# Attention with a gated unit on one core: heads of Q and K interleaved on partitions, stacked operands copied by row pairs

## The chip, the cores and the metric

The kernel runs on one core of one Trainium2 chip. The metric is the time of one execution on the device in microseconds (us), the median of several runs. Beside it stands one profiled execution, whose trace gives the duration of every instruction, what each engine waited for, and what the DMA queue did. TensorE (PE) multiplies matrices, VectorE (DVE), ScalarE (ACT) and GpSimd (POOL) work element by element, and SyncE (SP) issues all the transfers of this kernel.

## What is computed

Attention over queries that are averaged in pairs, and a gated unit over all heads of a batch. Cut to what matters:

```python
# q, k, v: (8, 8, 1152, 64) fp32
q_pool = q.reshape(B, H, S // 2, 2, D).mean(axis=3)          # 576 queries
scores = np.matmul(q_pool, k.transpose(0, 1, 3, 2)) / np.sqrt(D)
attn = np.exp(scores - np.max(scores, axis=-1, keepdims=True))
x = np.matmul(attn / (attn.sum(-1, keepdims=True) + 1e-9), v)  # to (8, 576, 512)
h = np.maximum(x @ w_in, 0.0)                                # w_in (512, 1024)
u, g = h[..., :512], h[..., 512:]
g = (g - mean(g)) / np.sqrt(var(g) + 1e-6)
g = np.einsum('ts,bsd->btd', w_spatial, g) + b_spatial[None, :, None]
out = (u * g) @ w_out                                        # (8, 576, 512)
```

## The kernel before

The 64 heads are worked off in 32 pairs of heads. For a pair, Q and K lie transposed in SBUF, 64 rows (the head's dimension) for each head, 128 rows for both: head 0 on the lower 64 partitions, head 1 on the upper 64. fp32 products are made of fp16 pieces: `prep` scales Q and K, rounds them to a head (qn[:, 0], kn) and keeps the rest (qn[:, 1], and for K a tile klo).

The scores of one tile of 128 keys by 512 queries are two matmuls into one bank. The first (L904) contracts over 128 rows: khi holds kn of one head twice, once on each half of the partitions, and qhi holds qn's head on one half and qn's rest on the other. The second (L905) contracts over 66 rows: klo holds K's rest on 64 rows and the constant -2**15 on two more, and X (xq) holds qn's head on 64 rows and on two more (rows D and D + 1, D = 64) the maximum of each query's scores, split into two fp16 numbers. The maximum is thus subtracted by the matmul. These stacked operands have to be written across partitions, which only a transfer does: `copies` (L681 to L683) makes ten of them for a pair, `prep` two for klo (L671, L672) and, from the third pair on, two for Z (tile qz, L646 and L647), and `shift` two for the rows of maxima (L732, mr into X). That is sixteen for a pair. Q's rest and its copies go through one tile qn; kn has two, klo three (NSET), the others two.

`maxima` finds the maxima: a matmul of kn with Z (L699), where Z holds qn's head with the other head's rows set to zero, so that one matmul over all 128 rows gives one head's products; DVE reduces each bank of 384 keys (L705). `shift` then takes the maximum over the banks (L718), subtracts and scales (L719), splits it in two (L722, L723), turns it by a matmul (L727), casts it to mr (L729) and sends it to X.

The main loop goes over the pairs i. During attention(i), the generators maxima(i + 1), prep(i + 2), split_v(i + 1) and the conversion of the weights run in steps beside it, and from pair 5 on the gated unit. At the start of a step come copies(i + 1) and the loads of pair i + 2. The first two pairs are prepared ahead of the loop and call `copies` from `prep`.

The program's order on each engine is not the order in which it is written: `Order.pin` lists all instructions, finds what each depends on, gives each a cost, and draws up one order for each of the five engines by a list schedule, SP's transfers among them. Each engine then runs strictly in that order. `Order.access` (L68) tells which rows and bytes of a tile an operand covers. On SP each transfer also waits until the eighth transfer before it has landed, since eight semaphores are handed round.

## Time and profile before

| | |
|---|---|
| median of 3 runs | 1170.97 us (1170.41 to 1171.24) |
| profiled execution | 1171.14 us |
| its span on the core | 1169.4 us |
| mean granted clock of TensorE | 0.997 |
| transfers by SP | 139.44 MB, 42.4% of the 16 DMA engines' time |

The span is what the trace covers; 1.7 us of the execution lie outside it. A row of a view names the line in the kernel, the engine, the operation and its tiles (written tile, arrow, read tiles). Rows that end in "<-" and a name tell what an idle engine waited for; the figures are the total in us, how often, and the longest. Rows of the chain hold a start, a length and the work that the end of the execution depended on at that time.

### The profile page before, as it was taken

To read this page: it belongs to the slowest core of one execution; us is meant where nothing else is said; L and a number is where in the kernel's file an instruction comes from. 1 tells how busy PE (TensorE), PEld (TensorE's weight loads), DVE (VectorE), ACT (ScalarE), POOL (GpSimd) and SP (SyncE) were. 2 spreads that over 40 slices of the span, in tenths; PEclk is the share of its full clock that TensorE was granted. 3 is DMA by queue.
4 is the path that set the end of the run, shared out by engine and by line. 5 is a ranking of instruction groups with operands and counts; after the bars stand their busy time and mean duration, and the time that the engine had idled before them with its cause. 6 is when DMAs were issued, how large, how long until landed. Compare 5 with 4: busy or idle time off the path is not lost.

```text
span 1169.4 us, 33651 instructions
## 1 busy us (share of the span) xinstructions
PE 1132.8 (97%) x13412; PEld 715.2 (61%) x13412; DVE 838.8 (72%) x2095; ACT 896.4 (77%) x1700; POOL 884.5 (76%) x766
## 2 busy tenths in 40 slices
PE   4999999999999999999999999999999999999998
PEld 1766676666566666666666666666666666665453
DVE  6899878898856877786668677865668676822644
ACT  7997899788886879797787977878777867754433
POOL 5765789879898889999987978888788977873000
PEclk9999999999999999999999999999999999999999
DMA  9855354345453344654533544366443432121002
GB/s 294 233 181 157 95 161 149 92 118 152 128 162 110 106 126 135 169 135 131 153 109 87 159 117 130 95 178 171 120 114 88 119 97 50 36 65 37 1 1 82
DMA packets 93757, 141.59 MB, mean 121 GB/s; under 512 B 36704, under 2 KB 52832, under 8 KB 93600
## 3 DMA queue, kind: packets, MB, share of 16 engines
q1 hardware_dynamic: 93600, 139.44, 42.4%
q8 instruction: 105, 1.72, 0.6%
q14 instruction: 52, 0.43, 0.1%
HBM read 81.20 MB, written 9.44 MB: 78 GB/s over the span
## 4 chain that ended last, share of the span: by engine, by line
PE 84%; DVE 10%; DMA 3%; ACT 2%; issue 1%; SPq 0%; DVEq 0%; ACTq 0%
PE pss L905 9%; PE pm L699 9%; PE pss L904 9%; PE pw L1002 7%; PE pw L1105 7%; PE pw L1149 6%; PE pw L1063 6%; PE o L807 5%; PE o L818 5%; PE o L813 5%; DVE mt L705 3%; PE o L800 2%; PE pss L921 1%; PE pm L878 1%; PE pm L876 1%; PE pss L1002 1%
## 5 line engine op out<-in xcount | busy, mean ns | idle before, releaser
L930 POOL TENSOR_TENSOR pt<-pt 128x512 f16<-128x512 f32 x546 | 597.6, 1113 | 128.8 <-ACT pt L910 126.7
L705 DVE TENSOR_REDUCE mt<-pm 128x1 f32<-128x384 f32 x762 | 404.4, 551 | 119.9 <-PE pm L699 114.5
L910 ACT ACTIVATE pt<-pss,esc 128x512 f32<-128x512 f32 x576 | 388.6, 694 | 112.0 <-PE pss L905 95.9
L699 PE MATMUL pm<-kn,qz 128*128 128x384 f16 x762 | 239.4, 329 | 6.9 <-DVE mt L705 4.5
L904 PE MATMUL pss<-qhi,khi 128*128 128x512 f16 x576 | 219.0, 381 | 4.2 <-ACT pt L910 1.8
L905 PE MATMUL pss<-xq,klo 66*128 66x512 f16 x576 | 218.5, 384 | 3.3 <-DMA xq<-mr 3.3
L807 PEld LDWEIGHTS <-pt 128*128 128x128 bf16 x2184 | 124.7, 98 | 61.4 <-issue 3.2
L807 PE MATMUL o<-vp,pt 128*128 128x65 f16 x2184 | 160.1, 193 | 0.5 <-DVE xm L826 0.4
L813 PE MATMUL o<-vp,pt 128*128 128x64 f16 x2184 | 158.8, 193 | 0.0
L818 PE MATMUL o<-vp,pt 128*128 128x65 f16 x2184 | 158.0, 193 | 0.2
L818 PEld LDWEIGHTS <-pt 128*128 128x128 f16 x2184 | 121.8, 98 | 52.3 <-POOL pt L930 1.8
L699 PEld LDWEIGHTS <-qz 128*128 128x128 f16 x864 | 83.8, 99 | 62.4 <-issue 19.1
L813 PEld LDWEIGHTS <-pt 128*128 128x128 bf16 x2184 | 105.6, 98 | 3.6 <-issue 0.2
L1002 PE MATMUL pw<-wi_h,xg 128*128 128x512 f16 x248 | 92.0, 379 | 0.0
L1063 PE MATMUL pw<-xg,wi_h 128*128 128x512 f16 (+2 forms) x368 | 82.9, 311 | 0.0
L930 POOL TENSOR_TENSOR ptl<-ptl 128x1152 f16<-128x1152 f32 x32 | 69.2, 2163 | 17.2 <-ACT ptl L926 17.2
L1149 PE MATMUL pw<-wo_h,vv 128*128 128x512 f16 x224 | 81.2, 379 | 0.5 <-DVE vv L402 0.3
L1105 PE MATMUL pw<-ws_h,vv 128*128 128x512 f16 x216 | 79.1, 379 | 0.7 <-DVE u L1115 0.7
L595 POOL TENSOR_TENSOR vp<-vt,vp 128x576 f16<-128x576 f32 x54 | 68.1, 1266 | 13.7 <-ACT vp L399 13.6
L905 PEld LDWEIGHTS <-klo 66*128 66x128 f16 x576 | 56.1, 98 | 34.6 <-issue 6.2
L926 ACT ACTIVATE ptl<-pss,esc 128x256 f32<-128x256 f32 (+1 forms) x128 | 64.5, 504 | 15.2 <-PE pss L921 15.2
L656 POOL TENSOR_TENSOR klo<-kt,kn 128x640 f16<-128x640 f32 (+1 forms) x54 | 72.7, 1348 | 0.0
(229 smaller groups left out, 2386.0 us busy)
## 6 DMA issues: line engine op xcount, KB each, us to landing
vt<-in_v_dram SPq DMA_DIRECT2D x56, 576.0 KB
qt<-in_qT_dram SPq DMA_DIRECT2D x32, 576.0 KB
khi<-kn SPq DMA_DIRECT2D x128, 144.0 KB
kt<-in_kT_dram SPq DMA_DIRECT2D x31, 576.0 KB
qhi<-qn SPq DMA_DIRECT2D x128, 72.0 KB
out_dram<-row SPq DMA_DIRECT2D x24, 256.0 KB
xq<-qn SPq DMA_DIRECT2D x64, 72.0 KB
klo<-klo SPq DMA_DIRECT2D x32, 144.0 KB
```

Source lines behind the costliest of these rows:

```text
L699: nc.tensor.matmul(pm[:, :W], lhsT=Z[:, t * P : (t + 1) * P], rhs=kn[:, n * NB : (n + 1) * NB, :], start=True, stop=True,)
L705: nc.vector.reduce_max(out=mt[:, t, n : n + 1], in_=pm[:, :W], axis=AX.X)
L807: nc.tensor.matmul(o[:, t], lhsT=top[:, cols], rhs=vp[:, D : D + D1], start=c == 0 and t == 0, stop=False, skip_group_check=True,)
L813: nc.tensor.matmul(o[:, t, 0:D], lhsT=top[:, cols], rhs=vp[:, 0:D], start=False, stop=False, skip_group_check=True)
L818: nc.tensor.matmul(o[:, t], lhsT=rst[:, cols], rhs=vp[:, D : D + D1], start=False, stop=c == NC - 1, skip_group_check=True,)
L904: nc.tensor.matmul(o, lhsT=khh[:, h, c, :], rhs=qhl[:, h, q], start=True, stop=False)
L905: nc.tensor.matmul(o, lhsT=KL[0:KR, h, c, :], rhs=X[0:KR, h, q], start=False, stop=True)
L910: nc.scalar.activation(pt, ps, AF.Exp, bias=0.0, scale=esc)
L930: nc.gpsimd.tensor_sub(t.bitcast(F16)[..., 0::2], t, t.bitcast(BF16)[..., 1::2])
L1002: nc.tensor.matmul(ph, lhsT=xa[:, cc, c0 : c0 + P], rhs=wa[:, cc, DH:DF], start=n == 0, stop=n == 3 * NCC - 1,)
L1063: nc.tensor.matmul(pu[:, : z - a], lhsT=wa[:, cc, fc * P : (fc + 1) * P], rhs=xa[:, cc, a:z], start=n == 0, stop=n == 3 * NCC - 1,)
L1105: nc.tensor.matmul(pv, lhsT=l, rhs=r[:, 0:MAIN], **fl)
```

## The change

Q's and K's rows are laid out as (dimension, head) in place of (head, dimension): row 2d + h holds dimension d of head h. The host hands them over in that order, and the loads stay whole tiles.

- The rows of one head are now every second partition. `copies` fills qhi of one head with one transfer from 64 rows, each of which gives two rows of the target (qn's head and its rest lie side by side in a row), and khi of one head with one transfer that reads each of the 64 rows of kn twice. X takes both heads in one transfer, and klo too. That is six transfers for what took ten and klo's two.
- K's rest goes to a tile of its own, kl, of which there is one; klo is filled from it by the last transfer of `copies`, is two tiles instead of three, and its rows of constants are set once at the start. prep's sums of squares use kn for their discarded output, not klo.
- Z is still written by two transfers, of every second row. For the first two pairs DVE multiplies all 128 rows by a column of ones and zeros (own), which is built from the identity matrix at the start, instead of copying 64 rows. Z is set to zero as a whole.
- The two rows of maxima go in one transfer (L733) instead of two.

A pair so has nine transfers (two for Z, six in `copies`, one for the maxima). `Order.access` is adapted to a step between rows.

```diff
@@ -73,8 +73,9 @@
             return None
         size = self.SIZE[ap.dtype]
         dims = [list(d) for d in ap.ap]
-        row, parts = dims[0]
+        row = math.prod(ap.tensor.shape[1:]) * self.SIZE[ap.tensor.dtype] // size
         first, off = divmod(ap.offset, row)
+        parts = dims[0][0] // row * (dims[0][1] - 1) + 1
         run, g, ext = size, 0, 0
         for s, n in sorted((d[0] * size, d[1]) for d in dims[1:] if d[1] > 1 and d[0]):
             if s == run and not g:
@@ -277,7 +278,7 @@
 def attn_sgu_kernel(ctx: ExitStack, tc: tile.TileContext, qT, kT, v, w_in, w_spT, b_sp, w_out, out):
     nc = tc.nc
     P = 128
-    B, NHP, _, D, _, S = qT.shape
+    B, NHP, D, _, _, S = qT.shape
     NC = kT.shape[4]
     NP = B * NHP
     KEYS = NC * P
@@ -345,9 +346,10 @@
 
     NSET = 3
     kns = [const.tile([P, NC, P], F16, name=f"kn{i}") for i in range(2)]
-    klo = [const.tile([P, 2, NC, P], F16, name=f"klo{i}") for i in range(NSET)]
+    kls = [const.tile([P, NC, P], F16, name=f"kl{i}") for i in range(1)]
+    klo = [const.tile([P, 2, NC, P], F16, name=f"klo{i}") for i in range(2)]
     for t in klo:
-        nc.gpsimd.memset(t[D:KR, 1], -MROW)
+        nc.gpsimd.memset(t[D:KR], -MROW)
     qns = [const.tile([P, 2, S], F16, name=f"qn{i}") for i in range(1)]
     xq = [const.tile([P, 2, S], F16, name=f"xq{i}") for i in range(2)]
     khi = [const.tile([P, 2, NC, P], F16, name=f"khi{i}") for i in range(2)]
@@ -355,8 +357,10 @@
 
     qz = [const.tile([P, 2, S], F16, name=f"qz{i}") for i in range(2)]
     for t in qz:
-        nc.gpsimd.memset(t[D:P, 0], 0.0)
-        nc.gpsimd.memset(t[0:D, 1], 0.0)
+        nc.gpsimd.memset(t, 0.0)
+    own = const.tile([P, 2], F32, name="own")
+    for h in range(2):
+        nc.vector.reduce_sum(out=own[:, h : h + 1], in_=ident[:, h::2], axis=AX.X)
 
     wi_h = const.tile([P, NCC, DF], F16, name="wi_h")
     wi_l = const.tile([P, NCC, DF], F16, name="wi_l")
@@ -508,13 +512,13 @@
 
         b, hp = divmod(i, NHP)
         qt = ld.tile([P, KEYS], F32, name="qt", bufs=2)
-        nc.sync.dma_start(out=qt, in_=qT[b, hp].rearrange("h d r s -> (h d) (r s)"))
+        nc.sync.dma_start(out=qt, in_=qT[b, hp].rearrange("d h r s -> (d h) (r s)"))
         state[i] = {"qt": qt}
 
     def load_k(i):
         b, hp = divmod(i, NHP)
         kt = mo.tile([P, NT * DH], F32, name="u")[:, :KEYS] if i == 1 else ld.tile([P, KEYS], F32, name="kt")
-        nc.sync.dma_start(out=kt, in_=kT[b, hp].rearrange("h d c p -> (h d) (c p)"))
+        nc.sync.dma_start(out=kt, in_=kT[b, hp].rearrange("d h c p -> (d h) (c p)"))
         state[i]["kt"] = kt
 
     v_first = {}
@@ -606,14 +610,14 @@
     def prep(i):
         st = state[i]
         kt, qt = st["kt"], st["qt"]
-        X, KL, khh, qhl, Z, kn, qn = (x[i % len(x)] for x in (xq, klo, khi, qhi, qz, kns, qns))
+        X, KL, khh, qhl, Z, kn, qn, kl = (x[i % len(x)] for x in (xq, klo, khi, qhi, qz, kns, qns, kls))
         k0 = kt.rearrange("p (c k) -> p c k", k=P)
         q0, q1 = qt[:, 0:S], qt[:, S:]
-        st.update(qhl=qhl, khh=khh, X=X, KL=KL, kn=kn, qn=qn, Z=Z)
+        st.update(qhl=qhl, khh=khh, X=X, KL=KL, kn=kn, qn=qn, Z=Z, kl=kl)
         first = i == 0
         (nc.vector if i < FIRST else nc.gpsimd).tensor_add(q0, q0, q1)
         sq = sm.tile([P, 2], F32, name="sq", bufs=2)
-        junk = KL[:, 0].rearrange("p c k -> p (c k)")
+        junk = kn.rearrange("p c k -> p (c k)")
         square_sum(sq[:, 0:1], kt, junk)
         yield
         square_sum(sq[:, 1:2], q0, junk[:, :S])
@@ -634,17 +638,16 @@
                 out=lnp, in0=lnp, scalar1=math.log(PEXP) / ESC, scalar2=2.0 ** 29, op0=ALU.mult, op1=ALU.min
             )
 
-        lower, upper = slice(0, D), slice(D, P)
         if not first:
             factors()
             yield
         head(qn[:, 0], q0, s_q)
         if i < FIRST:
-            nc.vector.tensor_copy(out=Z[lower, 0], in_=qn[lower, 0])
-            nc.vector.tensor_copy(out=Z[upper, 1], in_=qn[upper, 0])
+            for h in range(2):
+                nc.vector.tensor_scalar_mul(Z[:, h], qn[:, 0], own[:, h : h + 1])
         else:
-            nc.sync.dma_start(out=Z[lower, 0], in_=qn[lower, 0])
-            nc.sync.dma_start(out=Z[upper, 1], in_=qn[upper, 0])
+            for h in range(2):
+                nc.sync.dma_start(out=Z[h::2, h], in_=qn[h::2, 0])
         if not first:
             rest(qn[:, 1], q0, s_q, qn[:, 0])
             yield
@@ -653,34 +656,33 @@
                 nc.scalar.activation(k0[:, a:z], k0[:, a:z], AF.Copy, bias=0.0, scale=s_k)
                 yield
                 head(kn[:, a:z], k0[:, a:z], 1.0)
-                nc.gpsimd.tensor_sub(KL[:, 0, a:z], k0[:, a:z], kn[:, a:z])
+                nc.gpsimd.tensor_sub(kl[:, a:z], k0[:, a:z], kn[:, a:z])
             else:
                 head(kn[:, a:z], k0[:, a:z], s_k)
                 yield
                 if not first:
-                    rest(KL[:, 0, a:z], k0[:, a:z], s_k, kn[:, a:z])
+                    rest(kl[:, a:z], k0[:, a:z], s_k, kn[:, a:z])
             yield
         if first:
             rest(qn[:, 1], q0, s_q, qn[:, 0])
             factors()
             for a, z in ((0, 5), (5, NC)):
                 nc.scalar.activation(k0[:, a:z], k0[:, a:z], AF.Copy, bias=0.0, scale=s_k)
-                nc.gpsimd.tensor_sub(KL[:, 0, a:z], k0[:, a:z], kn[:, a:z])
+                nc.gpsimd.tensor_sub(kl[:, a:z], k0[:, a:z], kn[:, a:z])
         if i < FIRST:
             copies(i)
-        nc.sync.dma_start(out=KL[lower, 1], in_=KL[upper, 0])
-        nc.sync.dma_start(out=KL[D:KR, 0], in_=KL[D:KR, 1])
         yield
 
     def copies(i):
 
-        khh, kn, qhl, qn, X = (state[i][n] for n in ("khh", "kn", "qhl", "qn", "X"))
+        khh, kn, qhl, qn, X, KL, kl = (state[i][n] for n in ("khh", "kn", "qhl", "qn", "X", "KL", "kl"))
+        flat = "p c k -> p (c k)"
         for h in range(2):
-            rows = slice(h * D, (h + 1) * D)
-            for r in range(2):
-                nc.sync.dma_start(out=qhl[r * D : (r + 1) * D, h], in_=qn[rows, r])
-                nc.sync.dma_start(out=khh[r * D : (r + 1) * D, h], in_=kn[rows])
-            nc.sync.dma_start(out=X[0:D, h], in_=qn[rows, 0])
+            twice = kn[h::2].rearrange(flat).unsqueeze(1).to_broadcast([D, 2, KEYS])
+            nc.sync.dma_start(out=qhl[:, h], in_=qn[h::2])
+            nc.sync.dma_start(out=khh[:, h].rearrange(flat), in_=twice)
+        nc.sync.dma_start(out=X[0:D].rearrange("p h s -> p (h s)"), in_=qn[:, 0])
+        nc.sync.dma_start(out=KL[0:D].rearrange("p h c k -> p (h c k)"), in_=kl.rearrange(flat))
 
     def maxima(i):
         st = state[i]
@@ -727,9 +729,8 @@
         nc.tensor.matmul(t, lhsT=mc, rhs=ident_h, start=True, stop=True)
         mr = sm.tile([2 * NT, P], F16, name="mr", bufs=2)
         nc.vector.tensor_copy(out=mr[: 2 * n], in_=t[: 2 * n])
-        for r in range(2):
-            rows = X[D + r : D + r + 1].rearrange("p h s -> p (h s)")
-            nc.sync.dma_start(out=rows[:, a * P : z * P], in_=mr[r * n : (r + 1) * n])
+        rows = X[D : D + 2].rearrange("p h s -> p (h s)")
+        nc.sync.dma_start(out=rows[:, a * P : z * P], in_=mr[: 2 * n])
         yield
 
 
@@ -1286,6 +1287,7 @@
     NC = S2 // 128
 
     kT = k.reshape(B, H // 2, 2, 128, NC, D).transpose(0, 1, 2, 5, 4, 3)
+    qT, kT = (x.swapaxes(2, 3) for x in (qT, kT))
     return {
         "qT": qT,
         "kT": kT,
```

The planner draws up a new order. On SP, from the last copies of pair 0 (counted from 0) up to its first rows of maxima (mr into xq), before the change; klo_109 and xq_116 are operands of pair 0, qt and kt the loads of pair 2:

```order
L682 DMA khi_118<-kn_107 64x1152
L683 DMA xq_116<-qn_115 64x576
L671 DMA klo_109<-klo_109 64x1152
L511 DMA qt<-in_qT_dram 128x1152
L517 DMA kt<-in_kT_dram 128x1152
L672 DMA klo_109<-klo_109 2x1152
L455 DMA vv<-in_w_in_dram 128x2x512
L732 DMA xq_116<-mr 1x5x128 x2
```

And at the same place with the change, from the first copy of pair 0 on (klo_110 and xq_115 are pair 0's):

```order
L684 DMA xq_115<-qn_114 64x2x576
L683 DMA khi_117<-kn_107 128x1x1152
L682 DMA qhi_119<-qn_114 128x1x576 x2
L683 DMA khi_117<-kn_107 128x1x1152
L515 DMA qt<-in_qT_dram 128x1152
L685 DMA klo_110<-kl_109 64x2x1152
L521 DMA kt<-in_kT_dram 128x1152
L459 DMA vv<-in_w_in_dram 128x2x512
L544 DMA vt<-in_v_dram 128x2x576
L733 DMA xq_115<-mr 2x5x128
```

A load of V (vt) now stands ahead of the first rows of maxima, and the load of Q ahead of the copy to klo.

On DVE, from the reduction over the banks to the cast to mr of pair 2 (near 80 us in the trace of before) and somewhat beyond, before:

```order
L718 TENSOR_REDUCE pw<-mt 128x9
L719 TENSOR_SCALAR pw<-pw,lnp 128x9
L402 SCALAR_TENSOR_TENSOR klo_109<-kt,qks,kn_108 128x512
L722 CAST wide_135<-pw 128x9
L723 TENSOR_TENSOR wide_135<-pw,wide_135 128x9
L425 TENSOR_SCALAR vv<-vv 128x1024
L729 CAST mr<-pw 18x128
L705 TENSOR_REDUCE mt<-pm 128x1
L402 SCALAR_TENSOR_TENSOR vp_101<-xg,vs,vp_101 128x9x64
```

With the change:

```order
L720 TENSOR_REDUCE pw<-mt 128x9
L883 TENSOR_SCALAR xt<-pm,dent 64x64 x2
L721 TENSOR_SCALAR pw<-pw,lnp 128x9
L724 CAST wide_135<-pw 128x9
L725 TENSOR_TENSOR wide_135<-pw,wide_135 128x9
L406 SCALAR_TENSOR_TENSOR kl_109<-kt,qks,kn_108 128x512
L731 CAST mr<-pw 18x128
L395 TENSOR_REDUCE vt<-vsq 128x1
L406 SCALAR_TENSOR_TENSOR vp_101<-xg,vs,vp_101 128x9x64
L433 SCALAR_TENSOR_TENSOR vv<-vv 128x1024
L707 TENSOR_REDUCE mt<-pw 128x1
```

A step of the weights' conversion (L425, 1024 columns) has left the stretch ahead of the cast, two products for xt have come into it, and no reduction of maxima (mt) follows the cast at once.

On DVE again, at the same place of the next pair (near 112 us), before:

```order
L402 SCALAR_TENSOR_TENSOR wi_l<-u,wvs,wi_h 128x2x512
L882 TENSOR_SCALAR xt<-pm,dent 64x64 x2
L718 TENSOR_REDUCE pw<-mt 128x9
L719 TENSOR_SCALAR pw<-pw,lnp 128x9
L722 CAST wide_136<-pw 128x9
L723 TENSOR_TENSOR wide_136<-pw,wide_136 128x9
L402 SCALAR_TENSOR_TENSOR wi_l<-u,wvs,wi_h 128x2x512
L729 CAST mr<-pw 18x128
```

With the change:

```order
L720 TENSOR_REDUCE pw<-mt 128x9
L707 TENSOR_REDUCE mt<-pw 128x1
L721 TENSOR_SCALAR pw<-pw,lnp 128x9
L406 SCALAR_TENSOR_TENSOR kl_109<-kt,qks,kn_107 128x512
L724 CAST wide_136<-pw 128x9
L725 TENSOR_TENSOR wide_136<-pw,wide_136 128x9
L406 SCALAR_TENSOR_TENSOR vp_102<-xg,vs,vp_102 128x9x64
L731 CAST mr<-pw 18x128
L406 SCALAR_TENSOR_TENSOR wi_l<-u,wvs,wi_h 128x2x512
```

The two wide steps of the weights (wi_l) stood on both sides of the reduction; one now stands behind the cast, and a step of K's rest (kl) and one of V (vp) ahead of it.

## The prediction

> **What bounds the kernel now.** I read the page's totals first, then the windows of the stages, then the chain and the waits of TensorE.
>
> ```profile
> span 1169.4 us, 33651 instructions
> PE 1132.8 (97%) x13412; PEld 715.2 (61%) x13412; DVE 838.8 (72%) x2095; ACT 896.4 (77%) x1700; POOL 884.5 (76%) x766
> PE 84%; DVE 10%; DMA 3%; ACT 2%; issue 1%; SPq 0%; DVEq 0%; ACTq 0%
> ```
>
> TensorE is busy 97% of the span and holds 84% of the chain that ended last. The change takes no matmul away, so it can only recover what TensorE loses, 36.6 us of idle time (1169.4 - 1132.8), and what it loses by running slowly. The next view gives each stretch of the span with its length and busy times; the figure behind POOL is the granted clock, the last two are DMA.
>
> ```profile
> core 0: us, PE busy (x) PEld busy (x) DVE busy (x) ACT busy (x) POOL busy (x), PEclk, DMA share, GB/s
> 0.00:20.00 20.00, 8.02 (x24) 2.55 (x25) 12.86 (x30) 14.85 (x32) 9.57 (x20) 1.00 0.91 300
> 20.00:40.00 20.00, 15.32 (x123) 8.71 (x122) 16.55 (x47) 16.07 (x34) 10.08 (x9) 1.00 0.90 271
> 84.00:88.00 4.00, 2.24 (x29) 1.28 (x30) 3.58 (x8) 3.50 (x9) 1.19 (x2) 1.00 0.53 138
> 88.00:92.00 4.00, 4.00 (x37) 2.64 (x36) 4.00 (x8) 3.53 (x8) 1.95 (x2) 0.57 0.10 25
> 112.00:116.00 4.00, 3.30 (x37) 2.14 (x34) 3.90 (x9) 2.57 (x5) 1.04 (x1) 1.00 0.34 78
> 116.00:120.00 4.00, 2.75 (x18) 1.44 (x18) 4.00 (x11) 0.44 (x1) 0.00 (x0) 0.86 0.24 56
> 120.00:124.00 4.00, 4.00 (x47) 2.67 (x45) 2.99 (x7) 3.17 (x7) 2.09 (x2) 0.72 0.00 0
> 940.00:960.00 20.00, 20.00 (x246) 12.94 (x244) 15.62 (x37) 14.97 (x29) 16.08 (x14) 1.00 0.30 77
> ```
>
> The last row stands for most of the span: nothing is lost there. The loss sits in three places: the first 40 us (16.7 us idle), the stall at 84 to 88 (1.76 us idle), and the one at 112 to 120 (0.70 + 1.25). Behind each of the latter two the granted clock falls, to 0.57 and to 0.86 and 0.72, which costs 4 x 0.43 = 1.7 us and 4 x (0.14 + 0.28) = 1.7 us more. A stall here is paid twice. Which waits involve a transfer:
>
> ```profile
> PE pss L905 <- DMA xq<-mr: 3.3, 3, 1.9
> PE pss L904 <- DMA khi<-kn: 1.3, 1, 1.3
> 13.12 5.37 DMA khi<-kn
> 18.58 1.01 PE pss L904 x2
> ...
> 23.20 5.38 DMA xq<-mr
> 28.62 1.01 PE pss L905 x2
> ...
> 83.33 2.79 DMA xq<-mr
> 86.26 0.59 PE L905 MATMUL pss<-xq,klo 66*128 66x512 f16 x2 [1.09 <-DMA xq<-mr]
> 87.83 0.38 PE L904 MATMUL pss<-qhi,khi 128*128 128x512 f16 x1 [0.55 <-ACT pt L910]
> ...
> 474.65 3.44 DMA xq<-mr
> ```
>
> All of TensorE's waits on transfers are 4.6 us: one for the stacked K copies, three for the rows of maxima (mr into X, before the first L905 of a pair).
>
> **The change part by part.** *The start.* L905 at 28.62 is the gate: TensorE runs in order, so what is behind it waits too. It waits for the first rows of maxima, issued at 23.20 and 5.38 us under way, because they queue behind what was issued earlier. The rate of that queue:
>
> ```profile
> 3.00:9.00 6.00, 0.16 (x1) 0.00 (x0) 2.29 (x7) 2.73 (x7) 4.68 (x8) 1.00 1.02 395
> 14.50:18.50 4.00, 2.76 (x6) 0.48 (x5) 4.00 (x9) 3.94 (x10) 0.25 (x1) 1.00 0.99 212
> ```
>
> Loads over 128 rows move at 395 GB/s, the 64-row copies at 212, with the queue full in both. Ahead of the first rows of maxima the order of the change puts one more load (vt, 128 x 1152 of 4 bytes, 0.59 MB: 1.5 us at 395) and a klo copy of 64 x 2304 of 2 bytes, 0.29 MB, in place of half as much (+0.7 us at 212). Against that, 0.88 MB of khi and qhi go in 128-row transfers. No row shows an SBUF copy of that form: between 212 and 395 GB/s it saves 0 to 1.9 us. I take 395, since the loads are the only other 128-row transfers here: 1.5 + 0.7 - 1.9 = **+0.3 us**, at worst +2.2. L904 comes 1.0 us earlier by the same rate (it needs half of them) and gains nothing while L905 stays.
>
> The Trainium skill, "SBUF — State Buffer", section on the DMA port swizzle, says that a transfer's rate goes by how many of 16 ports its partitions reach, 64 consecutive ones reaching 8. The 212 against 395 agree; every second partition reaches all 16, so the rule gives the +0.3, while destinations X and klo, 64 consecutive rows, stay slow.
>
> The other edits of the start are covered:
>
> ```profile
> L643 DVE COPY qz<-qn x2: 292/297/302, 9.9 to 23.8; 64x576 f16<-64x576 f16 x2
> L1036 DVE TENSOR_SCALAR row<-vv,mv,rs x37: 527/544/1266, 220.9 to 1107.4; 128x512 f32<-128x512 f32 x37
> L350 POOL MEMSET klo<- x3: 1052/1101/1169, 1.9 to 4.0; 2x1152 f16 x3
> 7.50 0.34 POOL L407 MEMSET wide<- 128x128 f16 x2
> ```
>
> The masked products into qz take between 0.30 us each, as the copies did, and 0.59 (527 ns for 512 columns, scaled to 576); I take 0.35, nearer the f16 row. At worst 0.6 us on two, hidden by the queue that holds the copies until 14.5; without that cover it would be 0.6. The klo memsets are four of L350's size, not three: POOL ends 1.1 us later than 7.84, before qz is needed at 9.9. The two sums of ident are two reductions that DVE does before the first load lands.
>
> *The second gate, 86.26.*
>
> ```profile
> 82.44 1.64 SPq L732 DMA_DIRECT2D xq<-mr  x2
> 78.85 0.23 DVE L719 TENSOR_SCALAR pw<-pw,lnp 128x9 f32<-128x9 f32 x1
> 82.14 0.27 DVE L729 CAST mr<-pw 18x128 f16<-18x128 f32 x1
> L425 DVE TENSOR_SCALAR vv<-vv 128x1024 int32<-128x1024 int32 x2 | 2.6, 1298 | 0.0
> L429 DVE SCALAR_TENSOR_TENSOR vv<-vv 128x1024 int32<-128x1024 int32 x1 | 1.5, 1508 | 0.0
> L402 DVE SCALAR_TENSOR_TENSOR klo<-kt,qks,kn 128x640 f16<-128x640 f32 (+1 forms) x4 | 4.2, 1061 | 0.0
> L402 DVE SCALAR_TENSOR_TENSOR vp<-xg,vs,vp 128x576 f16<-128x576 f32 x4 | 4.0, 1000 | 0.0
> L402 DVE SCALAR_TENSOR_TENSOR wi_l<-u,wvs,wi_h 128x1024 f16<-128x1024 f32 x2 | 4.2, 2082 | 0.0
> L882 DVE TENSOR_SCALAR xt<-pm,dent 64x64 f32<-64x64 f32 x6 | 1.7, 277 | 0.0
> ```
>
> Two issues took 1.64 us; one takes half, 0.8 less until the rows are off. In DVE's new order L425 (1.30) no longer stands ahead of the cast to mr, two xt (0.28 each) do: 0.7 us earlier. Together 1.5 us, more than the wait of 1.09; the 0.55 behind it follows from it. So 1.76 idle and 1.7 of clock, 3.4 us, can go. Late next is DVE: around the cast (0.27) it now has 5.5 us without a reduction of maxima (two xt, kl 1.06, vp 1.00, L429 1.51, five short ones at up to 0.23), where it had 3.6 (klo 1.06, L425 1.30, four short ones). TensorE's L699 waits for those reductions, 0 to 1.9 us; I take the middle, 1.0. **-2.4 us** (-3.4 to 0).
>
> *The third, 109 to 124.* DVE held 5.9 us without a reduction (two wi_l of 2.08, two xt, mr, four short ones). Now kl and vp stand ahead of mr and one wi_l behind it: 2.08 + 1.06 + 1.00 + 0.27 and three short ones, 5.1. I count the difference, **-0.8 us**, and keep 0 and -3.6 (0.70 + 1.25 idle, 1.7 clock) as ends.
>
> *The one at 474.* A single issue brings the rows 0.8 us earlier than its wait (3.3 less 1.9 and 1.09, some 0.4 us) needs: **-0.4 us**.
>
> The stacked row pair has a price the other way:
>
> ```profile
> L732 SPq DMA_DIRECT2D xq<-mr x68: 612/747/1191, 22.3 to 1032.8; - x68
> ```
>
> 68 issues become 34. The trace gives no price of a 256-byte row. Between nothing and that of a 2304-byte row (a khi copy, 0.147 MB at 212 GB/s, is 0.7 us for 64 rows on 16 engines, 0.17 each) lies 0 to 1.6 us if one engine must do nine in turn. I take nothing; those copies are the nearest row, but of nine times the bytes.
>
> The Trainium skill, "DMA: Bandwidth & Descriptors", section on why a DMA increments its semaphore by 16, says the number of engines is the largest up to 16 that divides the outer sizes of both sides. For two rows from 18 that is 2 engines, where nine rows had 9: it speaks against this edit, and no run here shows it; it gives the 1.6 us.
>
> *The rest of the span.* Seven issues fewer a pair, about 4 us of SP, bring nothing where SP is not waited for: TensorE loses nothing there. kl rests in one tile, so its next write waits for the copy to klo. Behind that write on DVE (POOL in later pairs) stand maxima, or the rests of pt that L818 needs.
>
> ```profile
> 57.74 1.21 SPq L683 DMA_DIRECT2D xq<-qn  x1
> 74.05 1.11 DVE L402 SCALAR_TENSOR_TENSOR klo<-kt,qks,kn 128x640 f16<-128x640 f32 x1
> ```
>
> The klo copy goes out right behind the X copy, which ended its issue at 58.95; the next write came at 74.05, 15 us later. With the longest transfer above (5.4 us) 9 us are left: nothing.
>
> Sum: 0.3 - 2.4 - 0.8 - 0.4 = **-3.3 us** from the profiled execution's 1171.14 (span and 1.7 us around it), 0.2 above the median of the runs, 1170.97. That is **1167.8 us**.
>
> **The rivals.** *Both stalls go, clock and all* (-3.4 - 3.6 - 0.4, nothing at the start): 1163.7. For it: a stall avoided keeps the clock. Against: DVE is busy 4.00 of 4 us around both, and its work is the same. *Hidden or moved*: TensorE's freed time goes into new waits of the same size on DVE, whose order the planner drew anew: 1171, within 1.5. For it: 10% of the chain is DVE. *Slower at the start*: if a transfer's time goes by its rows, not by what they reach, the copies save nothing (+2.2) and the row pair on two engines costs 1.6 less the 0.8 of an issue, so L905 opens 3.0 us later and the second gate gains nothing: 1174.1. It decides from a copy rate below about 250 GB/s. Against it: 395 GB/s for loads of 128 rows. *kl binds*: a write that waits 1 us in each of 30 pairs gives 1200; against it the 9 us.
>
> **How the numbers follow.** Forecast 0.47 (its own range 1165 to 1170), both stalls 0.12, hidden 0.23, slower start 0.13, kl 0.05. A measurement of this kernel can tell about 0.2%, 2.3 us. Of the forecast about 0.34 lies beyond that; with the 0.12 and 0.02 of the hidden case faster is 0.48. Same is 0.13 + 0.18, and slower 0.13 + 0.05 + 0.03. The range from 1163.5 to 1173.3 leaves out kl, most of the slower start and a little of the best case.
>
> **What would show it.** Right: L905's first wait ends between 28 and 30; no wait on a transfer near 86, the clock at 1.00 there; DMA above 300 GB/s while khi and qhi move. Wrong: the first rows of maxima landing after 30, a granted clock below 1 at a new place between 60 and 140, or POOL or DVE waiting on the klo copy.

## The result and the profile after

| | before | after |
|---|---|---|
| median of 6 executions each | 1170.69 us (1167.22 to 1172.39) | 1178.84 us (1176.34 to 1183.16) |
| profiled execution | 1171.14 us | 1179.84 us |
| its span | 1169.4 us | 1177.7 us |
| granted clock of TensorE, mean | 0.997 | 0.995 |

The ratio is 1.0077 (95% interval 1.0052 to 1.0101): slower by 8.2 us, and 5.5 us above the upper end of the range. The page of the changed kernel, totals and chain:

```profile
span 1177.7 us, 33350 instructions
PE 1133.5 (96%) x13412; PEld 715.6 (61%) x13412; DVE 854.6 (73%) x2097; ACT 899.4 (76%) x1700; POOL 883.4 (75%) x763
PE 78%; DVE 11%; ACT 5%; DMA 3%; issue 1%; POOL 1%; SPq 0%; ACTq 0%; DVEq 0%; POOLq 0%
```

TensorE's work is the same, and so is POOL's. DVE is busy 15.8 us longer (838.8 before) for two instructions more: its instructions took longer. Where TensorE lost the time is read from the windows of both kernels (start and end, length, busy time of PE, PEld, DVE, ACT and POOL, granted clock, DMA). First before, then after:

```profile
80.00:100.00 20.00, 17.87 (x193) 11.94 (x192) 18.51 (x38) 16.84 (x34) 10.54 (x9) 0.91 0.50 145
100.00:140.00 40.00, 37.26 (x429) 26.39 (x427) 36.33 (x88) 30.41 (x53) 26.01 (x21) 0.96 0.42 126
140.00:320.00 180.00, 173.81 (x2190) 113.97 (x2190) 152.38 (x362) 156.89 (x297) 152.12 (x123) 1.00 0.46 133
520.00:540.00 20.00, 20.00 (x280) 13.33 (x278) 11.96 (x36) 18.46 (x37) 19.79 (x20) 1.00 0.64 179
```

```profile
80.00:100.00 20.00, 19.37 (x233) 14.12 (x233) 18.88 (x45) 19.97 (x46) 13.68 (x11) 1.00 0.64 175
100.00:140.00 40.00, 38.29 (x490) 28.71 (x489) 38.78 (x91) 33.93 (x59) 30.10 (x23) 1.00 0.52 164
140.00:320.00 180.00, 171.38 (x2132) 111.32 (x2129) 152.91 (x357) 154.71 (x293) 149.24 (x121) 0.99 0.43 132
520.00:540.00 20.00, 12.41 (x157) 8.12 (x153) 14.72 (x13) 8.77 (x18) 12.68 (x13) 0.83 0.48 155
```

What a window loses is its length less busy time times clock. From 80 to 140 it was 3.7 + 4.2 us and is 0.6 + 1.7, so 5.6 us are won: both stalls went, and the clock no longer falls. From 140 to 320 it was 6.2 and is 10.3, so 4.1 are given back. From 520 to 540 nothing was lost, and now 9.7. Those three come to 8.2 of the 8.3 us between the spans; the clock is given to a hundredth, which leaves the middle one uncertain by some 0.9 us. What is to be explained is one place, so its timeline is read next, DVE and PE first, then POOL (start, length, instruction; in brackets the idle time before it):

```profile
520.73 0.27 DVE L731 CAST mr<-pw 18x128 f16<-18x128 f32 x1
520.93 9.28 DVE L406 SCALAR_TENSOR_TENSOR qn<-qt,qks,qn 128x576 f16<-128x576 f32 x1
530.12 1.01 DVE L707 TENSOR_REDUCE mt<-pw 128x1 f32<-128x384 f32 x2
...
531.65 0.48 PE L701 MATMUL pm<-kn,qz 128*128 128x384 f16 x1 [7.59 <-DVE mt L707]
```

```profile
521.05 1.16 POOL L659 TENSOR_TENSOR kl<-kt,kn 128x512 f16<-128x512 f32 x1
522.17 3.04 POOL L931 TENSOR_TENSOR pt<-pt 128x512 f16<-128x512 f32 x3
525.16 1.24 POOL L599 TENSOR_TENSOR vp<-vt,vp 128x576 f16<-128x576 f32 x1
526.36 2.04 POOL L931 TENSOR_TENSOR pt<-pt 128x512 f16<-128x512 f32 x2
528.35 1.23 POOL L599 TENSOR_TENSOR vp<-vt,vp 128x576 f16<-128x576 f32 x1
```

One instruction of DVE, the rest of Q of pair 17, takes 9.28 us, though it needs 0.8 where nothing holds it up (the gated kernel below shows it). When it starts, POOL is in the last 0.1 us of an instruction; eight more follow end to end, the last until 529.58, and the rest ends at 530.21, 0.63 us later: it did its work only when POOL had nothing left to do. Meanwhile the reductions of maxima stand behind it on DVE, TensorE's L701 behind those, and everything else behind L701.

The Trainium skill, "SBUF — State Buffer", section "Who interferes with whom", says that a DVE instruction with two inputs from SBUF and a GpSimd instruction that reads SBUF contend for one shared pair of ports, that this is an exclusive lock, and that whichever issues first has it for its whole instruction while the other is blocked. The trace agrees that one waits for the other; that the wait goes on over eight further instructions is not in that rule.

### The profile page after: what moved, and what is told of

Its sections match the earlier page's. It is cut to its first block, busy times and chain, and to the rows that moved or that the text cites. A ratio compares the mean times of both kernels' runs of the same rounds, so it can differ in the third digit from the quotient of the medians.

```text
span 1177.7 us, 33350 instructions
## 1 busy us (share of the span) xinstructions
PE 1133.5 (96%) x13412; PEld 715.6 (61%) x13412; DVE 854.6 (73%) x2097; ACT 899.4 (76%) x1700; POOL 883.4 (75%) x763
## 4 chain that ended last, share of the span: by engine, by line
PE 78%; DVE 11%; ACT 5%; DMA 3%; issue 1%; POOL 1%; SPq 0%; ACTq 0%; DVEq 0%; POOLq 0%
PE pm L701 9%; PE pss L906 9%; PE pss L905 9%; PE pw L1150 6%; PE pw L1106 6%; PE pw L1064 6%; PE pw L1003 6%; DVE mt L707 5%; PE o L808 5%; PE o L819 4%; PE o L814 4%; DVE qn L406 2%; ACT pt L911 2%; PE pm L877 1%; PE pm L879 1%; PE pss L1003 1%
## 5 line engine op out<-in xcount | busy, mean ns | idle before, releaser
L701 PE MATMUL pm<-kn,qz 128*128 128x384 f16 x762 | 239.5, 330 | 14.2 <-DVE mt L707 13.5
L905 PE MATMUL pss<-qhi,khi 128*128 128x512 f16 x576 | 219.1, 381 | 3.1 <-ACT pt L911 1.2
L906 PE MATMUL pss<-xq,klo 66*128 66x512 f16 x576 | 218.3, 383 | 3.5 <-DMA xq<-mr 3.5
L701 PEld LDWEIGHTS <-qz 128*128 128x128 f16 x864 | 83.9, 99 | 64.0 <-issue 10.7
L906 PEld LDWEIGHTS <-klo 66*128 66x128 f16 x576 | 56.2, 98 | 43.9 <-issue 18.6
L659 POOL TENSOR_TENSOR kl<-kt,kn 128x640 f16<-128x640 f32 (+1 forms) x54 | 72.3, 1338 | 0.3 <-ACT kn L403 0.3
```

Source lines behind the costliest of these rows:

```text
L701: nc.tensor.matmul(pm[:, :W], lhsT=Z[:, t * P : (t + 1) * P], rhs=kn[:, n * NB : (n + 1) * NB, :], start=True, stop=True,)
L905: nc.tensor.matmul(o, lhsT=khh[:, h, c, :], rhs=qhl[:, h, q], start=True, stop=False)
L906: nc.tensor.matmul(o, lhsT=KL[0:KR, h, c, :], rhs=X[0:KR, h, q], start=False, stop=True)
```

## The experiments

Theory T: the order that the planner drew anew brings a long lock-out of one rest of Q (and, with it, the gains before 140 us), while the transfers cost nothing. Theory R: the transfers, or the single tile of K's rests, cost the time in any order. Kernels sent together ran on one chip; the medians of different groups come from different times and mostly from different chips, and the gated kernel below, sent three times, gave 1170.62, 1172.80 and 1171.42 us. So a difference of under some 2 us between groups says nothing.

### The same kernel again, and the event alone taken out

`e1_after_again` is the changed kernel. `e2_gate17` has its order on every engine, with one wait added after the order is fixed (shortened):

```diff
+            marks[i] = <rest of Q of pair i, on DVE>
...
-                nc.gpsimd.tensor_sub(kl[:, a:z], k0[:, a:z], kn[:, a:z])
+                nc.gpsimd.tensor_sub(kl[:, a:z], k0[:, a:z], kn[:, a:z])
+                if i == 17 and a:
+                    <this instruction waits for marks[i]>
```

> The changed kernel unaltered, for a second profile. Theory T (order): the loss is one event, the rest of Q of pair 17 on DVE, which POOL's gap-free train keeps from running for some 9 us; it recurs in the same place (a rest of over 6 us between 515 and 535 us), and the time is 1177 to 1180. Theory R (transfers): the loss is spread over the pairs or sits in the copies; then a second profile need not show the long rest, and the time is the same 1178. If the long rest is absent and the time is still 1178, T falls.

> Order of every engine as in the changed kernel; one wait added: POOL's second half of K's rest of pair 17 starts only after DVE's rest of Q of pair 17. T: the 9.28 us rest becomes 0.8 to 1.7 us, L701's wait of 7.6 us near 531 and the clock's fall to 0.83 go, and the time falls by 7 to 9 us, to 1169 to 1171.5. R (transfers, or the single tile of K's rests): nothing but some tenths of a us changes, 1177.5 to 1180.

Medians of 12 executions: 1180.61 us (1176.66 to 1183.76) and 1170.62 us (1169.11 to 1176.48), a ratio of 0.9915 (interval from resampled medians 0.9907 to 0.9926). The rest in the first, then the rest, POOL's gated half and the window in the second:

```profile
521.90 9.26 DVE L406 SCALAR_TENSOR_TENSOR qn<-qt,qks,qn 128x576 f16<-128x576 f32 x1
```

```profile
521.38 0.80 DVE L406 SCALAR_TENSOR_TENSOR qn<-qt,qks,qn 128x576 f16<-128x576 f32 x1
522.26 1.16 POOL L663 TENSOR_TENSOR kl<-kt,kn 128x512 f16<-128x512 f32 x1 [0.71 <-DVE qn L406]
```

```profile
520.00:540.00 20.00, 18.41 (x266) 12.32 (x262) 12.11 (x31) 15.41 (x32) 17.13 (x17) 1.00 0.63 189
```

A wait of 0.71 us on POOL is worth 10.0 us of the kernel. That the event is the cause of the loss is shown: nothing else differs, and every engine keeps its order.

### Operations and order apart

`e3_new_ops_old_order` has all edits of the change, but each of TensorE, DVE, ACT and POOL runs in the order of the kernel before, instruction by instruction (the two have the same instructions there, but for two sums at the start). `e4_old_ops_new_order` is the reverse. SP's order is drawn by the planner in both. In the planner, in part:

```diff
             for e, ns in ready.items():
+                if e in line:
+                    ns = [n for n in line[e][-1:] if n in ns]
```

> All the edits of the change (layout, row pairs, stacked copies, single tile of K's rests), but TensorE, DVE, ACT and POOL run in the order of the kernel before, instruction by instruction; only SP's order is drawn anew. T: the transfers by themselves cost nothing: no rest of over 3 us, and 1167.5 to 1171.5 (the gain of 6 us between 60 and 140 came with the new order as well, so it may be absent). R: the edits carry the loss whatever the order: 1176 to 1180.

> The operations and transfers of the kernel before, but TensorE, DVE, ACT and POOL in the order of the changed kernel; SP's order drawn anew. T: the order carries both the gain of some 4 to 6 us between 60 and 140 and the long rest near 520: 1174 to 1180 if DVE's rest starts within the same tenth of a us as POOL's train, 1165 to 1170 if it does not. R: 1169.5 to 1172, as before, and neither of the two shows in the trace.

Medians: 1175.26 us (1171.10 to 1181.24) and 1202.43 us (1198.20 to 1211.38). The longest rest of Q in each, e3 and then e4:

```profile
543.29 2.71 DVE L421 SCALAR_TENSOR_TENSOR qn<-qt,qks,qn 128x576 f16<-128x576 f32 x1
```

```profile
549.68 9.24 DVE L417 SCALAR_TENSOR_TENSOR qn<-qt,qks,qn 128x576 f16<-128x576 f32 x1
```

The lock-out comes along with the new order: it is in the old operations too, 9.24 us at the same pair. That the one profile of e3 has none shows less: the kernel before, in that same old order, has the event in about half of its executions (below), and three of e3's twelve lie at 1178.9 to 1181.2. As forecasts of times both theories miss. The new operations in the old order are 4.6 us above e2, whose order fits them, and the old ones in the new order 22 us above e1, which has the lock-out too: in an order made for other transfers, TensorE waits for transfers and for ACT behind them (3.4 us for a load of K at one place in e4). So the planner's order is not merely drawn anew; it is fitted, and neither half of the change can be judged in the other's order.

### The kernel before has the event too

While e1 to e4 ran, the kernel before stood at 1167 to 1175 us in 9 executions and at 1181 to 1188 in 20. It was therefore profiled again.

> The kernel before, unaltered, for a second profile: on the chip of the first four runs most of its times lay at 1181 to 1188 and the others at 1167 to 1175. Theory T (order, and DVE's rest shut out by POOL): the higher group is the same event, so a profile of over 1180 shows a rest on DVE of more than 6 us; a profile of about 1171 shows none over 3 us. If a profile of over 1180 shows no long rest, the two groups have another cause, which stays open.

The profiled execution took 1182.24 us. DVE and POOL around pair 17's rest, first in this execution and then in the first profile of before (1171.14 us):

```profile
514.69 10.97 DVE L402 SCALAR_TENSOR_TENSOR qn<-qt,qks,qn 128x576 f16<-128x576 f32 x1
...
513.56 4.03 POOL L930 TENSOR_TENSOR pt<-pt 128x512 f16<-128x512 f32 x4
517.55 1.40 POOL L656 TENSOR_TENSOR klo<-kt,kn 128x640 f16<-128x640 f32 x1
```

```profile
517.35 1.19 DVE L402 SCALAR_TENSOR_TENSOR qn<-qt,qks,qn 128x576 f16<-128x576 f32 x1
...
515.88 4.55 POOL L930 TENSOR_TENSOR pt<-pt 128x512 f16<-128x512 f32 x4
```

In the first profile the rest got in between two of the four pt (POOL's four took 4.55 us, not 4.03). In this one it did not, and waited to the end of the train, at the same instruction of the same order. Over all groups the kernel before ran 141 times: 74 times at 1167.1 to 1176.2 (median 1172.0), 67 times at 1178.9 to 1189.1 (median 1184.8), never between. All six executions of the kernel before in the result are of the lower group, and that is luck: on the chip of e1, 20 of its 29 executions were of the upper group, and its median there, 1183.27, is above the 1180.61 of the changed kernel. Two gated kernels test this: `e10_before_gate17` is the kernel before with the gate on POOL's first half of K's rest of pair 17, and `e11_gate17_again` is e2 beside it.

> The kernel before in its own order on all engines, with one wait: POOL's first half of K's rest of pair 17 starts only after DVE's rest of Q of that pair, which bounds a lock-out of 11 us to some 3.5. T (the times of the kernel before above 1180 are the same event): its times fall into one group, 1168 to 1176, median 1171 to 1173. Rival (the upper group has another cause, and the long rest only goes with it): a third or more of the times stay above 1180.

> The changed kernel with the gate at pair 17, again, beside the gated kernel before on one chip: what the change is worth without the event in either. From the profiles (1169.1 and 1171.1): 0 to 3 us below the gated kernel before, both in one group of times; the prediction's sum without the event would be 3.3 below, the rival in which the gain is given back 0 to 1.5.

1173.25 us (1166.73 to 1177.11) and 1172.80 us (1169.67 to 1176.02), 12 executions each, while 12 of the 28 of the ungated kernel before on that chip lay above 1181. The upper group is gone, so the two groups are this one event. And the two gated kernels are equal: ratio 0.9996 (resampled, 0.9980 to 1.0018). Without the event the change is worth nothing that can be measured, within some 2 us either way; the 3.3 us of the prediction lie outside that.

### The rows of maxima in one transfer

The new operations in the old order showed waits of TensorE on mr where before there were none (1.19 us at 116.48). Theory M blamed the row pair; three kernels separate it. (That only a transfer writes across partitions, as said ahead, holds for the way this kernel fills X; the kernel itself turns the maxima by a matmul, L729 with the change, which crosses them.) `e6_old_order_two_rows` is e3, and `e7_gate17_two_rows` is e2, with two transfers of nine rows; `e8_before_row_pair` is the kernel before with one transfer, in its own order. In all three the planner draws SP's order anew; besides the rows it moves three transfers in e7, five in e8 and none in e6.

```diff
-        rows = X[D : D + 2].rearrange("p h s -> p (h s)")
-        nc.sync.dma_start(out=rows[:, a * P : z * P], in_=mr[: 2 * n])
+        for r in range(2):
+            rows = X[D + r : D + r + 1].rearrange("p h s -> p (h s)")
+            nc.sync.dma_start(out=rows[:, a * P : z * P], in_=mr[r * n : (r + 1) * n])
```

> All edits but one, in the order of the kernel before on TensorE, DVE, ACT and POOL: the rows of maxima go to X in two transfers again, nine rows each. Theory M (the row pair in one transfer is slower to land: 3.5 to 4.8 us where the trace shows it on the chain, against 1.8 to 3.4 for nine rows): the waits of TensorE on mr near 116, 145, 280 and 317 us (2.8 us in sum, and the clock behind them) go, and the time falls by 2 to 4 us against the same kernel with one transfer, to a profile of 1170 to 1172. Theory N (the 3 us come from the copies or the single tile): 1173.5 to 1175.5, and those waits stay.

> The changed kernel in its own order, with the gate at pair 17, and the rows of maxima in two transfers. M: the waits on mr at 28.0 (1.91) and 311.7 (1.32) shrink by 0.5 to 1.5 us each, and the time falls by 1 to 3 us against the gate alone, to 1167 to 1169.5. N: no difference beyond 0.7 us, 1169.5 to 1171.

> The kernel before, in its own order on the four engines, with that one edit alone: the rows of maxima as a row pair in one transfer. M: waits on mr appear near 116 and 145 us as in the new operations in the old order, and the fast runs stand 1.5 to 4 us above the kernel before. N: within 1 us of it. What the prediction said of this edit (0.8 us earlier at the second gate, 0.4 at 474): 1 to 3 us below it.

Medians 1184.27, 1175.85 and 1172.55 us (of e8's ten, six lie at 1169.9 to 1173.3, three at 1181 to 1188, and one, at 3940, is set aside). M finds no support: with two transfers the kernel is not faster but slower, by 3.0 us against e11 in the new order (same chip, another time; ratio 1.0026, resampled 1.0016 to 1.0037; e2 and e16, on other chips, are lower still), and by some 9 us against e3 in the old one (on another chip). The chain of waits at one place, e3 and then e6 (start, length, what):

```profile
112.32 4.03 DMA xq<-mr
116.35 0.14 issue
116.48 1.01 PE pss L921 x2
```

```profile
114.80 0.19 DVE mr L746
...
116.63 4.19 DMA xq<-mr
120.82 0.28 issue
121.10 1.01 PE pss L922 x2
```

SP issues four large copies right ahead of these rows: in e6 mr is ready at 114.99 and SP free at 116.63, in e3 at 111.19 and 112.32. The rows themselves take much the same time to land, here and at the three other places where both chains show them: 4.03, 3.63, 4.10 and 4.78 us as a pair in e3, 4.19, 5.20, 3.58 and 5.09 from the second of two in e6. That the one issue less makes the difference fits this, but was argued and not shown. In the kernel before, the row pair at the second gate took longer to land, and the saved issue did not quite pay for it:

```profile
81.53 4.34 DMA xq<-mr
```

That is 4.34 us after its only issue, against 2.79 after the second of two (83.33 in the prediction's rows), 1.55 us more for 0.8 us of issue saved, and the first gate opened at 27.02 (28.62 and 27.77 in the two profiles of before), with a load of V moved behind these rows. In sum e8's lower six have a median of 1171.5, about 1 us below the lower 19 of the kernel before on that chip (1172.5).

### The single tile of K's rests

`e12_gate17_two_kl` is e2 with two tiles, the order of all five engines unchanged; e16 and e17 repeat the pair on another chip.

```diff
-    kls = [const.tile([P, NC, P], F16, name=f"kl{i}") for i in range(1)]
+    kls = [const.tile([P, NC, P], F16, name=f"kl{i}") for i in range(2)]
```

> The same with two tiles for K's rests instead of one, the order on all engines unchanged. If the single tile costs nothing (as predicted): the same time within 0.7 us. If its writes wait for the copy (the rival in which the tile binds): 1 us or more below the gate alone.

> The changed kernel with the gate at pair 17 once more, beside the next: 1169.5 to 1173, no time above 1178.

> The gate with two tiles for K's rests, again. If the 1.85 us by which it lay below the single tile is real: 1 to 2.5 us below, the interval of the ratio of the two away from 1. If it was scatter: within 0.7 us.

With two tiles 1170.96 against 1172.80 us (e12 and e11), and 1169.89 against 1171.42 (e17 and e16): 1.8 and 1.5 us faster, ratios 0.9984 (0.9964 to 0.9992) and 0.9987 (0.9969 to 1.0001). One tile probably costs some 1.5 us; the second interval just reaches 1. No row shows where: of kl's 64 writes one waits on a transfer in e11, on POOL near 24.5 us, for 0.8 us, and none in the changed kernel itself; with two tiles that write comes no earlier (24.7 in e12).

### A gate at every pair

`e14_gate_all` puts e2's gate at every pair from pair 5 on.

> The changed kernel in its own order, with the gate of pair 17 at every pair from the fifth on: POOL's second half of K's rest starts only after DVE's rest of Q of that pair. If the lock-outs of the other pairs cost time as well (2.6 us long at most): 0.5 to 2 us below the gate at 17 alone, 1168.5 to 1170.5. If DVE's rest comes later than POOL's half in other pairs, POOL waits, and it is 1 to 5 us slower, 1171.5 to 1176.

1175.12 us (1172.46 to 1177.40). POOL's waits in it (total, times, longest):

```profile
POOL kl L663 <- DVE qn L406: 13.6, 7, 3.3
```

In six other pairs DVE's rest comes late, and POOL now waits for it. The kernel is still faster than the changed one without a gate, but some 2 to 4 us slower than with the gate at pair 17 alone (1170.6 to 1172.8 us, on other chips). A gate is worth its wait only where the lock-out strikes.

### What decides the lock-out

Three kernels of their own, with nothing of the computation in them: in each trial ACT releases POOL and DVE; POOL runs a train of 8 or 10 instructions of 128x512, DVE first reduces from PSUM for a time that changes from trial to trial, and then does one rest of 128x576. In short:

```diff
+        for j in range(TRAIN):
+            nc.gpsimd.tensor_sub(pd[j], f[j], hb)
+        nc.vector.reduce_max(out=mx[:, 1:2], in_=z1[:, :n], axis=AX.X)
+        nc.vector.scalar_tensor_tensor(out=qd, in0=src, scalar=one, in1=hd, op0=ALU.mult, op1=ALU.subtract)
```

> A kernel of its own; it leaves the whole computation out. 48 trials: ACT releases POOL and DVE together; POOL does a train of eight TENSOR_TENSOR of 128x512 (as pt) without a gap, DVE reduces two pieces of PSUM, the second 20 elements longer in each trial (some 20 ns), and then one SCALAR_TENSOR_TENSOR of 128x576 (as qn's rest), alone 0.7 us. Theory L (lock-out by phase): for most offsets against the start of the POOL instruction then running the rest gets in at the next boundary (0.8 to 1.8 us), and in a narrow band of offsets, some 0.1 to 0.2 us around a boundary, it is kept out to the end of the train (4 to 7.5 us). Theory B (one instruction blocks at most one other): no rest takes over 1.9 us at any offset, and the long rests of the kernel have another cause. Theory A (always to the end of the train): all rests end with the train.

> The scan again, the whole computation left out, closer to the kernel: POOL's train is ten instructions of 128x512 (nine with a bf16 operand as pt, the fifth with f16 as K's rest), each waiting for a release by ACT that came long before; 40 phases 25 ns apart, each in four kinds of company: none, ACT working through SBUF, three SBUF to SBUF copies on SP's queue, both. If company or the kind of wait decides the lock-out (theory C): in some kinds rests of 4 to 10 us appear, ending with the train, in others none. If the phase does (L): a few in every kind at the same phase. If neither: none over 1.9 us, and what decides it stays open.

> The second scan, the whole computation left out, at the one phase where a rest was shut out (15.83 us; DVE's piece of 504 elements): pieces of 476 to 511 elements, one element (some 1.04 ns) apart, in the four kinds of company, all of it twice: 288 trials. If a narrow band of phases decides (L): the lock-outs stand at neighbouring pieces and at the same ones in both passes; one band of n pieces is n times 1 ns wide. If company decides (C): only in trials with copies under way. If it is chance: scattered, some 1 to 5 of 288, and not at the same pieces in both passes.

In e9 all 48 rests took 0.81 to 1.80 us: they got in at the next boundary between two instructions of POOL's train, at every phase, but for two that came within 0.04 us of a boundary and got in at the one after. In e13 one of 160 did not. DVE's rests of two trials of the same phase, then POOL from the second one on:

```profile
933.21 1.40 DVE L67 SCALAR_TENSOR_TENSOR qd<-src,one,hd 128x576 f16<-128x576 f32 x1
...
956.47 15.83 DVE L67 SCALAR_TENSOR_TENSOR qd<-src,one,hd 128x576 f16<-128x576 f32 x1
```

```profile
955.00 5.59 POOL L55 TENSOR_TENSOR pd<-f,hb 128x512 f16<-128x512 f32 x5
960.54 1.15 POOL L55 TENSOR_TENSOR pd<-src,hb 128x512 f16<-128x512 f32 x1
961.65 3.37 POOL L55 TENSOR_TENSOR pd<-f,hb 128x512 f16<-128x512 f32 x3
964.99 1.15 POOL L55 TENSOR_TENSOR pd<-f,hp 128x512 f16<-128x512 f32 x1
966.10 5.59 POOL L55 TENSOR_TENSOR pd<-f,hb 128x512 f16<-128x512 f32 x5
```

The phase is the time from the start of the POOL instruction then running. The first rest starts 1.47 us after the start of POOL's row at 931.74, the second 1.47 us after that at 955.00. One gets in, the other waits until POOL goes idle at 971.69 and ends at 972.30. In e15, around this phase, 10 of 288 rests were shut out, all for 15.84 to 15.87 us, always to the end of POOL's queue; all with pieces of 478 to 500 elements, at scattered pieces, and only at one piece (497) in both passes. Eight of the ten were in trials with copies alone, two in those without company, none in the 144 with ACT at work; these started at another phase, so company and phase stay mixed there.

Phase does matter. All 11 rests that were shut out in the three scans had started 0.337 to 0.365 us after the start of the POOL instruction then running. Of the others, 104 started in that same stretch and got in; of the remaining 381 none was shut out. So in the scans the phase seems needed but is not enough. Nor does one phase serve for all: in the kernels the long rests started 0.87 to 0.89 us after the start of a pt (after, e1, e4), 0.13 (e5, pair 17) and 0.40 (e5, near 193). What decides is open. Why the order of the changed kernel seems to meet it each time (18 of 18 executions at 1176 or more, three of three profiles in that order show it) and that of the kernel before in half of them was not shown.

Missing one boundary does not mean missing all. In the changed kernel another rest starts 0.08 us ahead of one, misses it, and gets in at the next:

```profile
184.54 2.10 DVE L406 SCALAR_TENSOR_TENSOR qn<-qt,qks,qn 128x576 f16<-128x576 f32 x1
...
184.62 1.41 POOL L659 TENSOR_TENSOR kl<-kt,kn 128x640 f16<-128x640 f32 x1
185.98 3.57 POOL L931 TENSOR_TENSOR pt<-pt 128x512 f16<-128x512 f32 x3
```

In the scans 16 rests did the same, all within 0.12 us of the boundary that they missed.

## Why the prediction was wrong

The step that failed is **"The rest of the span"**, which put TensorE's loss there at nothing. It looked for what the change adds there (issues, the wait on kl) and not for what the new order does to instructions that stay: of two engines that exclude each other, one may now be kept waiting for a whole train. That was worth 10.0 us (e1 against e2), three times the forecast gain; another 4.1 us went into new waits from 140 to 320, likewise put at nothing. The trace of before hinted at the exclusion, in rests of Q of up to 2.44 us where 0.8 is normal:

```profile
540.90 2.44 DVE L402 SCALAR_TENSOR_TENSOR qn<-qt,qks,qn 128x576 f16<-128x576 f32 x1
...
540.62 2.11 POOL L930 TENSOR_TENSOR ptl<-ptl 128x1152 f16<-128x1152 f32 x1
```

That rest waited for the one POOL instruction under way, and no longer. The text read DVE as an engine with too much work, never as one that waits. The planner knows of the exclusion: `Order.pin` puts a DVE instruction with two operands in SBUF at the end of the POOL instruction then running. But it reckons with one instruction, never with a train, so an order that looks free of loss to it can hold a wait of 9 us.

The same event is why the base itself was uncertain: 1171.14 and the three times shown belonged to the lower of two groups, and even that group spans 9 us, where the prediction reckoned with 2.3 us as what a measurement can tell. That the measured loss is 8.2 us is therefore in part luck of the base; that the change brings no gain without the event is not. All the signs that the prediction named came out on its right side (the first gate at 28.66, no wait on a transfer near 86, the clock at 1.00 there, over 300 GB/s), and none of them looked past 140 us.

Point by point:

- *The start, +0.3.* Right within 0.3. L906 starts at 28.66, after 28.62; the wait of L905 ends 1.0 us earlier, as said, and nothing comes of it. The rows of maxima take 7.32 us from a single issue at 21.21 (5.38 from the second of two at 23.20), and from 20 to 40 us the transfers, loads among them, move 316 GB/s where they moved 271, above the 300 that the prediction asked for.

```profile
17.58 1.01 PE L905 MATMUL pss<-qhi,khi 128*128 128x512 f16 x2 [0.43 <-DMA qhi<-qn]
28.66 1.01 PE L906 MATMUL pss<-xq,klo 66*128 66x512 f16 x2 [2.55 <-DMA xq<-mr]
```

- *Second gate, -2.4, and third, -0.8.* The direction was right, the size too small: 3.1 and 2.5 us by the windows, with the clock at 1.00 in both. The rival in which both stalls go had this part.
- *474, -0.4.* From 460 to 480 TensorE loses 0.2 us, not 0.6: right. (The subtraction as written gives 0.3; the wait itself was 0.36.)
- *Hidden or moved, the rival.* It was right from 140 to 320, where 4.1 us are given back, much of it in a stretch where L701 waits for reductions, as the rival said, and the clock falls to 0.96 (280 to 320):

```profile
291.83 0.66 PE L701 MATMUL pm<-kn,qz 128*128 128x384 f16 x2 [1.31 <-DVE mt L707]
293.10 0.92 PE L1150 MATMUL pw<-wo_h,vv 128*128 128x512 f16 x2 [0.61 <-ACT vv L403]
```

```profile
280.00:320.00 40.00, 36.50 (x438) 22.26 (x435) 31.57 (x76) 34.79 (x68) 33.79 (x28) 0.96 0.40 117
```

 So the gains and the new waits nearly cancel, and without the event the kernel stands where that rival put it: 1170.6, 1171.4 and 1172.8 us with the gate, the last equal to the gated kernel before beside it. As a time that rival, 1171 within 1.5, holds for the first two and is passed by 0.3 us by the third; what neither it nor the forecast had is the lock-out.
- *The row pair, taken as nothing.* In the kernel before that was right within 1 us. With the new copies it was probably undervalued: going back to two transfers costs some 3 us (e7 against e11, sent at different times), where SP's issues stand in line just ahead of these rows. The price of up to 1.6 us more for the transfer itself, which the prediction had as the upper end and left out, is seen at one place (4.34 against 2.79, 1.55 more, e8 and before) and not at the four of e3 and e6. The Trainium skill, "DMA: Bandwidth & Descriptors", section "Why a DMA increments its semaphore by 16 and not by 1", gives the number of DMA engines that a transfer uses, from which the prediction had 2 for the row pair against 9; no run here shows that number.
- *kl in one tile, nothing.* Nearly: probably some 1.5 us, not the 29 of the rival.
- *Slower start.* Did not happen.

The fastest kernel of the study is e12's and e17's, the change with the gate at pair 17 and two tiles for K's rests: 1170.96 and 1169.89 us, 0.9924 and 0.9949 of the kernel before on the same chips (intervals 0.9889 to 0.9959 and 0.9914 to 0.9984). Nearly all of that is the event it avoids; against the lower group of before (median 1171.59 beside e17) 1.7 us are left.

## What to carry to other kernels

When a change lets a planner draw an order anew, look in the old trace for pairs of engines that exclude each other, and for the longest instance of each instruction beside its median: an instruction that once took three times its length can take twelve times with a few instructions moved. Before trusting a difference of less than one per cent, run the base often enough to see whether its times form one group. And one wait, placed where a train would shut out the engine that the bound depends on, can be worth more than the transfers saved; put at every like place it gave back some 2 to 4 of the 10 us.

## What was not expected of the hardware

A rest on DVE with two inputs from SBUF mostly gets in at the next boundary between two instructions of POOL's train, sometimes at the one after. Now and then it is kept out until POOL has nothing left, and then ends 0.6 us after POOL: 3.37 us over three instructions, the one already running included (e5, 193.44), 9.24 to 9.28 over nine, 10.97 over ten, 15.8 over fourteen. In the scans this befell 11 of 496 rests, at a phase at which others took 1.4 us.

```profile
193.44 3.37 DVE L402 SCALAR_TENSOR_TENSOR qn<-qt,qks,qn 128x576 f16<-128x576 f32 x1
```
